# Earlier weight loads, a new order of the q, k and v loads, and a wider search in the planner of a fused attention and mixer kernel

## The chip, the cores and the metric

The kernel runs on one core of a Trainium2 chip. The metric is the device time of one execution in microseconds (us), of which medians are quoted. Every kernel is run in rounds beside the kernel before, on the same chip. A ratio is the mean time of one kernel's fast runs over that of the other kernel's fast runs of the same rounds, so it is not quite the ratio of the medians that stand beside it. An interval is a 95% one. Profiled executions are with a mean granted clock (the share of its full clock that PE was given) of 0.99 or more, unless it is said otherwise.

## The reference

Eight batches of attention over eight heads, 576 positions and a head dimension of 64, with a causal mask and a decay bias from `s`; the result goes through two mixers, one over the positions (tokens) and one over the 512 channels:

```python
cum = np.cumsum(np.maximum(s, 0.0), axis=-1)
scores = q @ k.T / 8 + np.minimum(-(cum[..., :, None] - cum[..., None, :]), 0.0)   # causal
x = softmax(scores) @ v                             # to [8, 576, 512]
u = x + (relu(x.T @ w_tok1) @ w_tok2).T             # token mixing
out = u + relu(u @ w_ch1) @ w_ch2                   # channel mixing
```

(Shortened: transposes and shapes are left to the reader.)

## The kernel before

The kernel doesn't fix the order of its instructions. It states operations with what they read and write, the engines that may run them and an assumed duration; a planner, in Python, simulates them, chooses engine and order, and repeats that with perturbed priorities. The best order by the planner's own reckoning is what each engine gets. So a changed load can move every instruction.

```python
def run(self, passes=5, search=60):
    rng = random.Random(1)
    for i in range(passes + search):
        self.reset()
        if i >= passes:                     # five plain passes, then random ones
            for o in self.ops:
                o.tail = base[o] + (rng.gauss(0.0, 2.0) if rng.random() < 0.02 else 0.0)
        order, length = self.once(i > 0)
        if best is None or length <= best[0]:
            best = ...                      # cut
```

(The loop is shortened.) All loads go through one queue of SyncE, in the order in which they are stated. The engines' names below are PE (matmuls; PEld is its weight load), DVE, ACT and POOL; SPq is the queue of SyncE. The part that the change touches:

```python
stage_v(0, 0)                       # v of batch 0, heads 0 to 3, five chunks
quad(0, 0)
load_tok1(Buf(r_uTb))
stage_v(0, 1)                       # heads 4 to 7
quad(0, HQ)
...
load_tok2(Buf(r_x))                 # then cast to bf16 by ACT and POOL
sga, sv = Buf(r_ga), Buf(r_vf)      # staging buffers of the channel weights
load_ch1(sga, 0, 0); load_ch1(sga, 1536, 1); load_ch1(sv, 0, 2); load_ch1(sga, 0, 3)
stage_qk(1, 0);  load_ch2(sga, 1536, 0)
stage_qk(1, HQ); load_ch2(sv, 0, 1); load_ch2(sga, 0, 2)
v1 = stage_v(1); ...; load_ch2(sga, 1536, 3)
for b in range(2, B):               # v between the k and q loads of its batch
    stage_qk(b, 0); vb = stage_v(b); vb[0](); vb[1]()
    stage_qk(b, HQ, 0); vb[2](); vb[3](); stage_qk(b, HQ, 1); vb[4]()
```

(Several statements are put on one line here, and cuts are marked with "...".) After a load of q or k come a cast, a 32-block transpose on DVE, and on ACT a square with its sum (a check of the inputs' size, whose result is needed only much later). The chunks of v are multiplied by the decay on POOL or DVE before the attention-times-v matmuls.

## Time and profile before

| | before |
|---|---|
| median time | 290.41 us (3 runs, 289.9 to 290.91) |
| profiled span | 288.6 us |
| PE busy | 278.1 us, 96% |
| useful matmul work (columns at 2400 per us, fillers left out) | 251.7 us |
| start A, to the long run of channel matmuls of batch 0 | 27.16 us |
| stage B, to the point where 51.4 us of work are done | 45.27 us |
| stage C, to the last matmul | 211.95 us |
| tail | 4.2 us |

How the stages are cut, and the lines behind the table, are in the prediction below. PE is 90% busy in nearly every slice, so a gain must come from short waits of PE or from better packing, not from making something else faster. And in the first ten slices the DMA engines are as full as PE.

### The profile page before, as it was taken

The numbers are of one execution on the slowest core, as the hardware profiler recorded it, in microseconds if no ns is written. First come the engines' busy times: TensorE is split into PE (matmuls) and PEld (weight loads), VectorE is DVE, ScalarE is ACT, GpSimd is POOL, SyncE is SP. The second block draws the span as 40 slices with busy tenths as digits, with TensorE's granted clock in tenths as the row PEclk, the third lists the DMA queues.
The fourth block names the chain that finished last, engine by engine and source line by source line (L and its number), as shares of the span: only waits on it lengthen the run. The fifth ranks groups of instructions, "written<-read, shape, count | busy, mean of one in ns | idle before, by whom it ended". The sixth has DMA issues, their size and how long they took to land.

```text
span 288.6 us, 6564 instructions
## 1 busy us (share of the span) xinstructions
PE 278.1 (96%) x2544; PEld 155.7 (54%) x2574; DVE 174.6 (61%) x333; ACT 187.3 (65%) x354; POOL 91.8 (32%) x143
## 2 busy tenths in 40 slices
PE   8889999999999999999999999999999999999994
PEld 3665455456754545356754545456744545357543
DVE  4973785989999774696358586785245513640022
ACT  3876876998899478986894578847842264018500
POOL 4653022557537427631382104621212102000000
PEclk9999999999999999999999999999999999999999
DMA  7999999899659999999935965951005310160032
GB/s 231 296 283 355 405 293 305 229 326 313 145 169 294 159 332 298 273 203 264 315 62 101 299 225 165 283 144 39 2 0 93 127 39 0 55 148 36 2 101 86
DMA packets 68128, 54.07 MB, mean 187 GB/s; under 512 B 53760, under 2 KB 56640, under 8 KB 68096
## 3 DMA queue, kind: packets, MB, share of 16 engines
q1 hardware_dynamic: 68096, 53.64, 66.7%
q8 instruction: 21, 0.34, 0.5%
q14 instruction: 11, 0.09, 0.1%
HBM read 40.65 MB, written 9.44 MB: 174 GB/s over the span
## 4 chain that ended last, share of the span: by engine, by line
PE 75%; DMA 11%; SPq 6%; ACT 3%; DVE 3%; issue 1%; DVEq 0%; ACTq 0%
PE pmx L1137 29%; PE pmx L1111 27%; DMA qkf<-in_q_dram 6%; PE pmx L803 5%; PE psc L759 4%; SPq L635 4%; PE pmx L1028 4%; DMA vf<-in_v_dram 4%; PE pmx L1053 4%; DMA x<-in_moe_w_tok_dram 2%; PE psc L923 1%; SPq L680 1%; DVE qkb L701 1%; PE pmx L965 1%; PE pmx L1036 1%
## 5 line engine op out<-in xcount | busy, mean ns | idle before, releaser
L776 ACT ACTIVATE E<-psc 128x512 bf16<-128x512 f32 x120 | 63.6, 601 | 25.1 <-PE psc L759 22.5
L784 POOL TENSOR_SCALAR_AFFINE_SELECT E<-E 128x512 bf16<-128x512 bf16 (+1 forms) x65 | 38.0, 614 | 96.3 <-ACT E L776 74.4
L1111 PEld LDWEIGHTS <-wc 128*128 128x128 bf16 x528 | 50.8, 98 | 31.9 <-issue 0.9
L1137 PE MATMUL pmx<-wc,gb 128*128 128x512 bf16 (+1 forms) x244 | 53.8, 369 | 0.5
L1111 PE MATMUL pmx<-uTb,wc 128*128 128x320 bf16 x384 | 54.0, 299 | 0.0
L1117 ACT ACTIVATE gb<-pmx 128x320 bf16<-128x320 f32 x80 | 34.6, 443 | 23.5 <-PE pmx L1111 17.6
L647 POOL TENSOR_TENSOR vp<-vf,wT 128x512 bf16<-128x512 f32 (+2 forms) x35 | 34.8, 1012 | 19.9 <-DMA vf<-in_v_dram 13.8
L685 ACT ACTIVATE junk<-qkf 128x1152 bf16<-128x1152 f32 x32 | 37.5, 1171 | 4.2 <-DMA qkf<-in_k_dram 3.9
L1137 PEld LDWEIGHTS <-gb 128*128 128x128 bf16 x252 | 23.8, 98 | 25.4 <-issue 0.9
L1137 PE MATMUL pmx<-wc,ga 128*128 128x512 bf16 x137 | 32.9, 379 | 0.4
L1111 PE MATMUL pmx<-uTa,wc 128*128 128x512 bf16 x141 | 31.8, 379 | 0.2
L803 PEld LDWEIGHTS <-E 128*128 128x128 bf16 x576 | 20.9, 97 | 6.4 <-issue 2.0
L817 DVE TENSOR_TENSOR x<-pmx,rc 128x320 bf16<-128x320 f32 x48 | 23.1, 489 | 1.4
L1117 ACT ACTIVATE ga<-pmx 128x512 bf16<-128x512 f32 x27 | 16.1, 597 | 11.5 <-PE pmx L1111 11.5
L1145 DVE TENSOR_TENSOR of<-pmx,ub 128x512 f32<-128x512 f32 (+1 forms) x17 | 11.2, 658 | 20.0 <-PE pmx L1137 18.1
L714 DVE STREAM_TRANSPOSE kT<-qkb 128x576 f32<-128x576 f32 x16 | 20.0, 1253 | 3.4 <-PE psc L759 2.3
L1137 PEld LDWEIGHTS <-ga 128*128 128x128 bf16 x144 | 13.1, 98 | 15.5 <-issue 1.5
L714 DVE STREAM_TRANSPOSE qT<-qkb 128x576 f32<-128x576 f32 x16 | 19.9, 1246 | 0.7 <-POOL qkb L699 0.4
L759 PE MATMUL psc<-qT,kT 32*128 32x256 bf16 (+2 forms) x592 | 19.1, 251 | 1.1 <-DVE qT L714 1.0
L759 PEld LDWEIGHTS <-kT 32*128 32x128 bf16 x640 | 13.6, 92 | 9.5 <-issue 7.6
L701 DVE CAST qkb<-qkf 128x1152 bf16<-128x1152 f32 (+1 forms) x22 | 15.1, 700 | 4.1 <-DMA qkf<-in_k_dram 2.7
L812 DVE RECIPROCAL rc<-pmx 128x5 f32<-128x5 f32 x48 | 8.7, 184 | 14.2 <-PE pmx L803 13.7
(115 smaller groups left out, 295.0 us busy)
## 6 DMA issues: line engine op xcount, KB each, us to landing
qkf<-in_k_dram SPq DMA_DIRECT2D x20, 576.0 KB, 6.1
qkf<-in_q_dram SPq DMA_DIRECT2D x20, 576.0 KB, 6.4
out_dram<-of SPq DMA_DIRECT2D x31, 256.0 KB, 2.5
vf<-in_v_dram SPq DMA_DIRECT2D x28, 256.0 KB, 6.0
ga<-in_moe_w_ch_dram SPq DMA_DIRECT2D x6, 768.0 KB, 7.6
vf<-in_v_dram SPq DMA_DIRECT2D x15, 128.0 KB, 5.3
vf<-in_moe_w_ch_dram SPq DMA_DIRECT2D x2, 768.0 KB, 10.3
out_dram<-of SPq DMA_DIRECT2D x10, 128.0 KB, 2.4
```

Of the source, the lines that this page charges most:

```text
L647: eng.tensor_tensor(out=vp.t[0:n, c, h0:h1, 0:D], in0=vf.t[0:n, c, h0:h1, :], in1=wT[0:n, c, b * H + h0 : b * H + h1].unsqueeze(2).to_broa ...
L685: P.op({"ACT": (1.1, 1.5, lambda: nc.scalar.activation(out=junk[:, :], in_=f.t[:, :], func=AF.Square, accum_out=sq[:, col : col + 1]))}, r ...
L701: nc.vector.tensor_copy(out=o.t[:, a:z], in_=i.t[:, a:z])
L714: nc.vector.transpose(out=T.t[:, 0:S, :].rearrange("p s q -> p (s q)").bitcast(FP32).rearrange("p (t r) -> p r t", r=R), in_=t1.t[:, :].bi ...
L759: nc.tensor.matmul(out=ps[e].t[:, c0 : c0 + z - a], lhsT=kT.t[p0 : p0 + TP, jc * 128 : jc * 128 + 128, qq], rhs=qT.t[p0 : p0 + TP, a:z, qq ...
L776: nc.scalar.activation(out=E.t[:, e, ph * 512 : ph * 512 + 512], in_=p.t[:, :], func=AF.Exp, scale=0.125)
L784: nc.gpsimd.affine_select(out=w, in_=w, compare_op=ALU.is_ge, fill=0.0, base=0, pattern=[[0, HQ], [1, n]], channel_multiplier=-1)
L803: nc.tensor.matmul(out=o[:, ic, 0 : D + 1], lhsT=E.t[:, hh, d0 : d0 + 128], rhs=vp.t[:, jc, h + hh, 0 : D + 1], start=(jc == j_lo), stop=( ...
L817: nc.vector.tensor_tensor(out=x.t[:, :, (h + hh) * D : (h + hh + 1) * D], in0=o[:, :, 0:D], in1=rc.t[:, :].unsqueeze(2).to_broadcast([128, ...
L1111: nc.tensor.matmul(out=pm.t[:, 0 : e - a], lhsT=wc1[:, m, cc * 128 : cc * 128 + 128], rhs=uT.t[:, m, a:e], start=(m == 0), stop=(m == NMC ...
L1117: lambda cc=cc, pm=pm, a=a, e=e: nc.scalar.activation(out=g.t[:, cc, a:e], in_=pm.t[:, 0 : e - a], func=AF.Relu),
L1137: nc.tensor.matmul(out=pm.t[:, na:nb], lhsT=g.t[:, cc, c * 128 : c * 128 + 128], rhs=wc2[:, cc, na:nb], start=(cc == 0), stop=(cc == NCC - 1))
```

## The change

The intent was to have each load land nearer to its use: the second token weight ahead of three v chunks, a third staging buffer for the channel weights, channel weight 2 among the v chunks of batch 1, and from batch 2 on q and k ahead of v. The planner gets a wider search, and a scan on DVE becomes a short reduction. The core of the diff (of the search only its heart, of the check nothing is shown; the comment is added):

```diff
-    def run(self, passes=5, search=60):
+    def run(self, passes=5, search=100):
...
+                if mode > 0.4:                      # also move whole groups of matmuls
+                    for g in sorted({p[0] for p in ranks.values()}):
+                        if rng.random() < 0.1:
+                            trial[g] = trial.get(g, 0.0) + rng.gauss(0.0, 0.7)
...
-    stage_v(0, 1)
+    vh = stage_v(0, 1)
+    vh[0]()
+    vh[1]()
+    load_tok2(Buf(r_x))
+    vh[2]()
+    vh[3]()
+    vh[4]()
     quad(0, HQ)
...
-    load_tok2(Buf(r_x))
-    sga, sv = Buf(r_ga), Buf(r_vf)
+    sga, sv, sv2 = Buf(r_ga), Buf(r_vf), Buf(r_vf)
...
-    load_ch1(sga, 0, 3)
+    load_ch1(sv2, 0, 3)
...
+    load_ch2(sga, 1536, 1)
     v1[0]()
+    load_ch2(sv, 0, 2)
     v1[1]()
...
     for b in range(2, B):
         stage_qk(b, 0)
-        vb = stage_v(b)
-        vb[0]()
-        vb[1]()
-        stage_qk(b, HQ, 0)
...
+        stage_qk(b, HQ)
+        for f in stage_v(b):
+            f()
```

More of the change, by code (lines that the diff above doesn't have):

```diff
@@ L50 @@
 RING = 2048
+SEED = 1
 class Plan:
@@ L155, in reset @@
             r.uses = []
-    def run(self, passes=5, search=60):
+    def run(self, passes=5, search=100):
         best = None
         self.lengths = []
-        rng = random.Random(1)
+        rng = random.Random(SEED)
         base = None
+        ranks = {o: o.prio for o in self.ops if isinstance(o.prio, tuple)}
+        moved = {}
         for i in range(passes + search):
@@ L164, in run @@
             if i >= passes:
+                mode = rng.random()
                 for o in self.ops:
-                    o.tail = base[o] + (rng.gauss(0.0, 2.0) if rng.random() < 0.02 else 0.0)
-            used = {o: o.tail for o in self.ops} if i else None
-            order, length = self.once(i > 0)
+                    o.tail = base[o] + (rng.gauss(0.0, 2.0) if mode < 0.7 and rng.random() < 0.02 else 0.0)
+                trial = dict(moved)
+                if mode > 0.4:
+                    for g in sorted({p[0] for p in ranks.values()}):
+                        if rng.random() < 0.1:
+                            trial[g] = trial.get(g, 0.0) + rng.gauss(0.0, 0.7)
+                for o, p in ranks.items():
+                    o.prio = (p[0] + trial.get(p[0], 0.0),) + p[1:]
+            used = {o: o.tail for o in self.ops} if i else None
+            try:
+                order, length = self.once(i > 0)
+            except RuntimeError:
+                if i < passes:
+                    raise
+                continue
             if best is None or length <= best[0]:
@@ L173, in run @@
                 base = used
+                if i >= passes:
+                    moved = trial
             self.lengths.append(round(length, 1))
@@ L492 @@
     PMASK = 1
+    LATER = True
     VUS = 1.05
@@ L615 @@
     junk = sb("junk", [128, R * D], BF16, fast)
-    pre = s_sb
+    pre = sb("pre", [64, 3], FP32, fast)
     gap = sb("gap", [64, 4], FP32, fast)
@@ L669, in stage_v @@
         todo = [lambda c=c, h0=h0, h1=h1: chunk(c, h0, h1) for (h0, h1) in parts for c in range(NJ)]
-        if b:
+        if b or part and LATER:
             return todo
@@ L1176 @@
     load_ch1(sv, 0, 2)
-    load_ch1(sga, 0, 3)
+    load_ch1(sv2, 0, 3)
     stage_qk(1, 0)
-    load_ch2(sga, 1536, 0)
+    load_ch2(sga, 0, 0)
     stage_qk(1, HQ)
-    load_ch2(sv, 0, 1)
-    load_ch2(sga, 0, 2)
     v1 = stage_v(1)
+    load_ch2(sga, 1536, 1)
     v1[0]()
+    load_ch2(sv, 0, 2)
     v1[1]()
@@ L1188 @@
     v1[4]()
-    load_ch2(sga, 1536, 3)
+    load_ch2(sga, 0, 3)
     for b in range(2, B):
         stage_qk(b, 0)
-        vb = stage_v(b)
-        vb[0]()
-        vb[1]()
-        stage_qk(b, HQ, 0)
-        vb[2]()
-        vb[3]()
-        stage_qk(b, HQ, 1)
-        vb[4]()
+        stage_qk(b, HQ)
+        for f in stage_v(b):
+            f()
     for b in range(2):
@@ L1210 @@
             chan0(tok0(), av0)
-    P.op({"DVE": (1.3, 1.6, lambda: nc.vector.tensor_tensor_scan(
-        out=pre[:, :], data0=one_sb[:, :].to_broadcast([64, S]), data1=wn[:, 0:S], initial=0.0, op0=ALU.mult, op1=ALU.add))},
+    P.op({"DVE": (0.5, 0.7, lambda: nc.vector.tensor_reduce(
+        out=pre[:, :], in_=wn[:, 0:384].rearrange("p (c n) -> p c n", n=128), op=ALU.add, axis=mybir.AxisListType.X))},
         reads=["wn", ("sq", 10)], writes=["pre"], prio=50)
@@ L1218, in gaps @@
             j = 128 * (i + 1)
+            if i:
+                nc.vector.tensor_tensor(out=pre[:, i : i + 1], in0=pre[:, i : i + 1], in1=pre[:, i - 1 : i], op=ALU.add)
             nc.vector.scalar_tensor_tensor(out=gap[:, i : i + 1], in0=wn[:, j + 128 : j + 129], scalar=4.8e-7,
-                                           in1=pre[:, j - 1 : j], op0=ALU.mult, op1=ALU.is_lt)
+                                           in1=pre[:, i : i + 1], op0=ALU.mult, op1=ALU.is_lt)
         nc.vector.tensor_scalar(out=gap[:, 3:4], in0=cum[:, S - 1 : S], scalar1=160.0, scalar2=None, op0=ALU.is_gt)
```

## The prediction

> **What bounds the kernel now.** I first read the busy times and the 40 slices, because the parts moved are loads of the first hundred microseconds and their limit may differ from the average.
>
> ```profile
> span 288.6 us, 6564 instructions
> PE 278.1 (96%) x2544; PEld 155.7 (54%) x2574; DVE 174.6 (61%) x333; ACT 187.3 (65%) x354; POOL 91.8 (32%) x143
> ...
> PE   8889999999999999999999999999999999999994
> DMA  7999999899659999999935965951005310160032
> GB/s 231 296 283 355 405 293 305 229 326 313 145 169 294 159 332 298 273 203 264 315 62 101 299 225 165 283 144 39 2 0 93 127 39 0 55 148 36 2 101 86
> ```
>
> PE is the bound, in nine tenths of every slice. The DMA row says that for the first ten slices (to about 72 us) the DMA engines are just as full, and that slack appears only from the eleventh on. So two limits stand side by side where the change acts.
>
> PE busy time hides small waits, so I set useful work against the clock. The program's matmuls are known by count and width. A steady stretch gives their rate: in the chain, 96 matmuls of 320 columns took 13.04 us, 135.8 ns each, which is 320 columns at 2400 per us plus 2.5 ns. Counting columns at 2400 per us, score matmuls (32 rows, L759) at a quarter because four run together, the two 64-row kinds at a half, and fillers (L1264) and the unused general branch at nothing, both kernels hold the same 251.7 us of useful work. Cut at two places of the PE timeline:
>
> ```profile
> 27.16 9.44 PE L965 MATMUL pmx<-uTa,wc 128*128 128x512 bf16 x42
> ...
> 49.79 1.78 PE L803 MATMUL psc<-vp,E 128*128 128x65 bf16 x45
> ...
> 58.55 1.90 PE L1053 MATMUL pmx<-h,w 128*128 128x512 bf16 x7
> ...
> 68.19 0.63 PE L759 MATMUL psc<-qT,kT 32*128 32x256 bf16 x16 [0.37 <-DVE qT L714]
> ...
> 72.43 7.23 PE L1111 MATMUL pmx<-uTb,wc 128*128 128x320 bf16 x52
> ```
>
> In program order 12.0 us of useful work precede the first of these rows and 51.4 us the last. So start A (0 to 27.16) loses 15.2 us; stage B (27.16 to 72.43) does 39.4 in 45.3 and loses 5.9; stage C (72.43 to the last matmul's end at 284.4) does 200.3 in 212.0 and loses 11.7; the tail, a last addition and store, is 4.2. These add to 288.6. C holds 1797 matmuls in 109 runs of one kind: 2.5 ns for each matmul is 4.5 us, and the other 7.2 us are 0.066 us for each change of kind. That is about what a stream without waits costs, so C has little to give. At C's rate (5.8%) B would lose 2.3; the other **3.6 us of B are real waits**. By the rows: 27.16 to 49.79 nothing to speak of (0.2), 49.79 to 55.55 about 1.0 (attention times v of batch 1), 55.55 to 63.29 about 1.4 (token mixing of batch 1), then about 1.0 to 72.43, of which 0.37 is the qT wait shown.
>
> For A I followed the chain of work that ended last:
>
> ```profile
> 15.41 4.86 DMA x<-in_moe_w_tok_dram
> 20.29 0.67 ACT w L850
> 20.96 1.04 ACT x L823 x5
> 22.05 1.03 PE psc L923 x10
> ```
>
> The load of w_tok2 is queued behind all v chunks of batch 0, lands at 20.29, and ACT, in order, must cast it (0.67) before it normalises the fourth head (1.04), which the next token matmul waits for. That is the link that the first part of the change attacks.
>
> **What the Trainium skill says.** "Perfetto Trace Analysis", section Identifying the Most-Contended Engine, says matmul busy share is no good measure of distance from the roofline; the trace agrees: stage B shows 43.55 us busy in 45.27, against 39.4 us of work. "TensorE: Matmul & The Clock Gate", section Wait — 56ns, not 53.3ns?, gives N/2.4 GHz plus about 2.5 ns per warm matmul; the 135.8 ns above agree. "DMA: Bandwidth & Descriptors", section Queues, rings and completion order, has one queue consumed in ring order on each DMA engine: moving a load forward pushes back what it passes; here all loads sit on one queue. The same page's Why small descriptors are slow charges a fixed cost per packet, heavy for 256 bytes; v rows are 256 bytes, and in the slices where v chunks move the rate is near 230 GB/s at full DMA busy share, against 355 to 405 with wide rows.
>
> **The change part by part.**
>
> *w_tok2 before v chunks 2 to 4 of heads 4 to 7.* Bytes are unchanged. The three chunks passed are 320 KB; at some 230 GB/s that is 1.4 us, so w_tok2 should land near 18.9 instead of 20.29, and the last v chunk near 20.3 instead of about 18.85 (where the last v multiplication of batch 0 begins). Gain: the cast and head 3 no longer hold anything. Loss: the four attention-times-v groups of heads 4 to 7, at 19.20 to 21.9 before, now start after v plus one multiplication (0.4 to 0.6), about 20.8, and end about 22.1 (36 matmuls took 1.26). In the new order heads 2 and 3's token matmuls come after them and a filler, about 22.3, against 22.05. Then four heads are normalised on DVE at 0.20 + 0.49 each, 2.7 us from about 21.3, ending near 24.0; the last token matmuls then start near 24.1 against 24.88. With the same 2.3 us to follow, the long run of channel matmuls starts about 26.6 instead of 27.16. **A: −0.5 us.** The fillers agree: the new program has 28 in place of 29, all at the same places but one.
>
> *Three staging buffers.* The third and fourth pieces of channel weight 1 go to the two v buffers, so the fourth no longer waits for a cast out of ga. That wait was 4.4 us in the DMA queue's own waits (L888 on ga), but in those microseconds the DMA engines ran at 0.9 to 1.07: the queue had work ahead. Direct gain about 0; it lets the k and q loads of batch 1 be queued some us earlier.
>
> *Channel weight 2 among v of batch 1; q and k ahead of v from batch 2.* Stage B's DMA is full, so nothing moves more bytes; only the order is nearer to the use. Before, q of batch 2 heads 4 to 7 was issued at about 61.9 behind v and its score matmuls waited at 68.19. Now k and q of a batch go together and that wait should vanish (0.4). The new PE order also puts three to six channel matmuls (0.65 to 1.3 us) between groups of attention times v, and three between the token matmuls and their continuation, where PE before ran 63 such matmuls in a row with DVE in between. I credit 0.7 of the first 1.0, 0.5 of the 1.4, 0.4 of the last 1.0. **B: −1.6 us.**
>
> *The planner's wider search and the shorter check.* Instructions of C change places, not number: 116 runs in place of 109, 7 × 0.066 = **+0.4 us** in C. The scan of 1.60 us on DVE at 76.55 becomes a reduction; DVE is no bound there: 0.
>
> Sum: −0.5 − 1.6 + 0.4 = −1.7; 290.4 − 1.7 = 288.7, and I write 288.6.
>
> **Rivals.** (1) *Hidden anyway.* With DMA full to 72 us, each load brought forward delays another: v of batch 2 now waits behind two 576 KB loads (about 1.7 us each at 350 GB/s), while its five POOL multiplications (1.04 us each) ended near 67 and are used from 70.40. That slack of 3.4 is just the delay, so B could gain only 0.5: 289.8 to 290.4. For it: the full DMA row. Against: k and q had cost a visible wait, v had not. (2) *A new wait.* The same delay overshoots, or v(0)'s later landing in A is not hidden; attention times v waits on the POOL multiplications, and PE is held up to 2 us: 291 to 292. For it: POOL already waited for v 13.8 us in all. Against: v is consumed a batch later than it is queued. (3) *All waits go.* If A gains 1.5 and B all 3.6: 285.3. Even this is 1.8%, so faster by over 2% (under 284.6) needs a gain in C, where no wait is seen.
>
> **Range and chances.** Between rival 3 softened and rival 2 softened: 286.4 to 291.0. Faster by over 2% has 0.03, slower by over 2% (over 296.2) 0.02, for a schedule whose assumed durations miss on the chip.
>
> **What would show it.** Right: w_tok2 lands before 19.5; the long L965 run (its new line) starts at 26.3 to 27.0; the score matmuls of batch 2 no longer name qT; the same 51.4 us of work are done near 70.3; the stretch to PE's end stays near 212. Wrong: PE waiting on attention times v behind POOL multiplications in 65 to 110 us; PE reaching the same work at 72 or later; C growing by over 1 us, which would mean that the search's new order, not the loads, decides.

## The result, and the profile after

The changed kernel took 289.46 us (median of 4 runs, 289.06 to 289.76), the kernel before in the same rounds 290.5 us (4 runs). The ratio is 0.9965, interval 0.9943 to 0.9987: about 1 us, a third of one per cent, "same" by the 2% line and inside the forecast range.

The page of the changed kernel answers to the lines shown of the kernel before:

```profile
span 287.9 us, 6550 instructions
PE 277.5 (96%) x2541; PEld 155.3 (54%) x2573; DVE 167.4 (58%) x330; ACT 183.3 (64%) x351; POOL 100.3 (35%) x151
...
PE   8899999999999999999999999999999999999994
...
DMA  7999998999568999549914978793007310280032
...
PE 87%; SPq 4%; issue 2%; DVE 2%; DMA 2%; ACT 1%; DVEq 0%; ACTq 0%
```

The last line is the head of the chain that ended last. Before, its first entries were PE 75%, DMA 11%; now DMA is 2% of it. The new order of loads did take the loads off the critical chain, and the time hardly moved. That contrast is the puzzle.

The same cuts through PE's timeline of the changed kernel (its lines are 19 to 21 further down than those of the kernel before: L984 was L965, L1130 was L1111, L822 was L803, L1047 was L1028, L778 was L759):

```profile
27.38 7.93 PE L984 MATMUL pmx<-uTa,wc 128*128 128x512 bf16 x35
...
49.24 1.25 PE L822 MATMUL psc<-vp,E 128*128 128x65 bf16 x36
...
54.57 1.90 PE L1047 MATMUL pmx<-x,w 128*128 128x512 bf16 x8
...
66.91 0.63 PE L778 MATMUL psc<-qT,kT 32*128 32x256 bf16 x16
...
71.41 7.78 PE L1130 MATMUL pmx<-uTb,wc 128*128 128x320 bf16 x56
```

The first row is the end of start A, and it has moved the wrong way, from 27.16. In the fourth row the wait on qT (0.37 before) is gone. In program order 50.88 us of work precede the last row, so the 51.4 us at which stage C was cut are reached about 0.55 later, at 71.96.

| stage | before | after | difference | forecast |
|---|---|---|---|---|
| A | 27.16 | 27.38 | +0.2 | -0.5 |
| B | 45.27 | 44.58 | -0.7 | -1.6 |
| C | 211.95 | 211.92 | 0.0 | +0.4 |
| tail | 4.2 | 4.0 | -0.2 | 0 |
| span | 288.6 | 287.9 | -0.7 | -1.7 |

Where did A's gain go? The next lines are a stretch of the changed kernel's timeline, all engines:

```profile
18.48 0.67 ACT L869 CAST w<-x 128x576 bf16<-128x576 f32 x1 [0.54 <-DMA x<-in_moe_w_tok_dram]
...
19.53 1.09 DVE L666 TENSOR_TENSOR vp<-vf,wT 128x256 bf16<-128x256 f32 x3 [1.68 <-DMA vf<-in_v_dram]
...
22.57 0.83 ACT L869 CAST wc<-ga 128x768 bf16<-128x768 f32 x1 [1.21 <-DMA ga<-in_moe_w_ch_dram]
...
23.46 0.10 PEld L984 LDWEIGHTS <-wc 128*128 128x128 bf16 x1 [0.40 <-ACT wc L869]
...
23.69 1.03 PE L942 MATMUL psc<-x,w 128*128 128x128 bf16 x10 [0.45 <-ACT h L949]
```

The second token weight lands by 18.48 (20.29 before), as forecast. But the v chunks behind it arrive later: the multiplication by the decay starts at 19.53, not at 18.17 as before. And PE's new order has the first channel matmul (the PEld row) ahead of the last twenty token matmuls. Its weight was still being cast by ACT, which itself waited 1.21 us for the load. PE stood until 23.46. The last row names the ReLU's `h` for its wait of 0.45; the weight-load row shows what stood in front. (That `h` was not needed is seen in the first experiment, where the same matmuls ran from 23.19 while ACT did its `h` from 23.34 on.)

In stage B the token mixing of batch 1 begins 1.0 us earlier (54.57 against 55.55), yet the channel matmuls behind it begin at 63.56, against 63.29. PE's timeline before, and then after:

```profile
55.55 1.90 PE L1028 MATMUL pmx<-x,w 128*128 128x512 bf16 x8
...
63.05 0.40 PE L1083 MATMUL pmx<-ident,us 128*128 128x128 bf16 x4 [0.31 <-DVE us L1070]
63.29 4.54 PE L1111 MATMUL pmx<-uTb,wc 128*128 128x320 bf16 x32
```

```profile
62.70 0.38 PE L1102 MATMUL pmx<-ident,ub 128*128 128x128 bf16 x4 [0.45 <-ACT uTb L1110]
63.19 0.38 PE L1102 MATMUL pmx<-ident,us 128*128 128x128 bf16 x4
63.56 3.42 PE L1130 MATMUL pmx<-uTb,wc 128*128 128x320 bf16 x24
```

From 54.57 to 63.56 are 8.99 us, before the same stretch took 7.74; 0.65 of the difference is three channel matmuls that the new order puts in between, so it is worse by 0.6. I read this at first as ACT's fault: in its order a square of q, 1.2 us long, stands at 60.88 ahead of the copies of uTb. The experiments below show that this reading was wrong.

### The profile page after: what moved, and what is told of

It is laid out like the page before. It is cut to its first block, busy times and chain, and to the rows that moved or that the text cites. A ratio compares the mean times of both kernels' runs of the same rounds, so it can differ in the third digit from the quotient of the medians.

```text
span 287.9 us, 6550 instructions
## 1 busy us (share of the span) xinstructions
PE 277.5 (96%) x2541; PEld 155.3 (54%) x2573; DVE 167.4 (58%) x330; ACT 183.3 (64%) x351; POOL 100.3 (35%) x151
## 4 chain that ended last, share of the span: by engine, by line
PE 87%; SPq 4%; issue 2%; DVE 2%; DMA 2%; ACT 1%; DVEq 0%; ACTq 0%
PE pmx L1130 29%; PE pmx L1156 29%; PE psc L778 5%; PE pmx L822 5%; PE pmx L1047 4%; PE pmx L984 4%; PE pmx L1007 3%; PE pmx L1072 3%; SPq L654 3%; DMA vf<-in_v_dram 2%; PE pmx L1055 1%; PE psc L822 1%; PE psc L942 1%; SPq L699 1%; DVE x L836 1%
## 5 line engine op out<-in xcount | busy, mean ns | idle before, releaser
L795 ACT ACTIVATE E<-psc 128x512 bf16<-128x512 f32 x120 | 63.1, 608 | 15.9 <-PE psc L778 12.0
L1130 PEld LDWEIGHTS <-wc 128*128 128x128 bf16 x528 | 50.6, 98 | 31.6 <-issue 1.3
L803 POOL TENSOR_SCALAR_AFFINE_SELECT E<-E 128x512 bf16<-128x512 bf16 (+1 forms) x65 | 38.3, 617 | 81.6 <-ACT E L795 58.8
L1130 PE MATMUL pmx<-uTb,wc 128*128 128x320 bf16 x384 | 54.0, 300 | 0.0
L1136 ACT ACTIVATE gb<-pmx 128x320 bf16<-128x320 f32 x83 | 36.2, 438 | 21.2 <-PE pmx L1130 14.2
L1130 PE MATMUL pmx<-uTa,wc 128*128 128x512 bf16 x139 | 32.7, 380 | 0.2
L1136 ACT ACTIVATE ga<-pmx 128x512 bf16<-128x512 f32 x23 | 13.7, 597 | 18.5 <-PE pmx L1130 18.5
L718 POOL CAST qkb<-qkf 128x1152 bf16<-128x1152 f32 (+1 forms) x15 | 14.7, 991 | 28.3 <-DVE kT L733 8.9
L822 PEld LDWEIGHTS <-E 128*128 128x128 bf16 x576 | 20.6, 97 | 5.5 <-issue 1.0
L778 PE MATMUL psc<-qT,kT 32*128 32x256 bf16 (+2 forms) x592 | 19.2, 252 | 1.3 <-DVE qT L733 1.3
L778 PEld LDWEIGHTS <-kT 32*128 32x128 bf16 x640 | 13.4, 92 | 10.3 <-issue 7.5
```

The lines of the kernel that those rows point to most:

```text
L718: nc.gpsimd.tensor_copy(out=o.t[:, a:z], in_=i.t[:, a:z])
L778: nc.tensor.matmul(out=ps[e].t[:, c0 : c0 + z - a], lhsT=kT.t[p0 : p0 + TP, jc * 128 : jc * 128 + 128, qq], rhs=qT.t[p0 : p0 + TP, a:z, qq ...
L795: nc.scalar.activation(out=E.t[:, e, ph * 512 : ph * 512 + 512], in_=p.t[:, :], func=AF.Exp, scale=0.125)
L803: nc.gpsimd.affine_select(out=w, in_=w, compare_op=ALU.is_ge, fill=0.0, base=0, pattern=[[0, HQ], [1, n]], channel_multiplier=-1)
L822: nc.tensor.matmul(out=o[:, ic, 0 : D + 1], lhsT=E.t[:, hh, d0 : d0 + 128], rhs=vp.t[:, jc, h + hh, 0 : D + 1], start=(jc == j_lo), stop=( ...
L1130: nc.tensor.matmul(out=pm.t[:, 0 : e - a], lhsT=wc1[:, m, cc * 128 : cc * 128 + 128], rhs=uT.t[:, m, a:e], start=(m == 0), stop=(m == NMC ...
```

## The experiments

**The method.** For seven of the twelve runs the changed kernel's plan was kept as it is ("frozen") and single operations were given another place in it before the instructions were emitted. So a difference is that of the edit and not of a new draw of the planner. The other five change what the planner is given.

**Theory.** The loads came in time, and the gain was lost where an in-order engine had a wrong instruction ahead of the one that PE needed: in A the first channel matmul, in B the squares on ACT. **The DMA rival** (rival 1 of the prediction): the loads are hidden or collide anyway, since DMA is full. **The search rival**, which the forecast named only as what a growth of C would mean: the search's draw decides, not the loads.

### First channel matmul behind the last token matmuls

```diff
     order = P.run()
+    keep_op["ch", 0, 0].start = keep_op["ch", 1, 0].start - 0.005
+    order.sort(key=lambda o: (o.start, o.idx))
```

> The changed kernel with one PE operation moved: the first channel matmul of batch 0 (L984, one of 512 columns) goes from ahead of the last token matmuls of batch 0 to behind them; every other instruction keeps its place. Theory (that matmul's weights are still being cast by ACT until 23.40, and PE, in order, stands 0.45 us at it): the token matmuls x20 start near 23.25 instead of 23.69, the long run of channel matmuls near 26.9 instead of 27.38, and the time is some 0.4 us under the changed kernel's, about 289.0 (ratio to before 0.995). Rival (the relu on ACT, which the list of waits names, or the normalisation on DVE holds them): start stays at 23.6 to 23.7 and 27.3 to 27.4, time 289.5 (0.9965).

It took 290.22 us, ratio 0.9969 (0.994 to 0.9999). The twenty token matmuls began at 23.19 in place of 23.69 and without a wait, and the long run of channel matmuls at 26.89 in place of 27.38. Of these 0.49 us, 0.22 is the matmul that moved, so 0.27 is real, and as 0.28 it was still there at 63.28 and 71.13. So the starts came as the theory said; the time did not (ratio 0.9969 for some 0.995). By 82 us the gain had vanished. DVE's cast of batch 4's first k in the changed kernel, and then all engines near 80 us in this one:

```profile
78.01 0.98 DVE L720 CAST qkb<-qkf 128x1152 bf16<-128x1152 f32 x1
```

```profile
78.65 1.23 DVE L722 CAST qkb<-qkf 128x1152 bf16<-128x1152 f32 x1 [0.75 <-DMA qkf<-in_k_dram]
...
79.79 0.18 DVE L833 RECIPROCAL rc<-pmx 128x5 f32<-128x5 f32 x1
...
81.89 0.49 DVE L838 TENSOR_TENSOR x<-pmx,rc 128x320 bf16<-128x320 f32 x1
...
82.44 0.81 PE L1051 MATMUL pmx<-x,w 128*128 128x512 bf16 x3 [0.43 <-DVE x L838]
```

Here DVE had to wait 0.75 us for the load of that k; in the changed kernel it did not wait. The normalisation of batch 2, for which PE waits, stands behind it in DVE's order. Token mixing of batch 2 started at 82.44, in the changed kernel at 82.23. The 0.28 won turned into 0.21 lost. Most of this is not that DVE came early: the load was issued at 73.5 and took 5.2 to land, in the changed kernel at 72.8 and 5.0. The five v chunks ahead of it in the queue took 10.19 us to issue (from 63.15), in the changed kernel 9.26 (from 63.42). So a late load took the gain back in this execution, as the DMA rival has it, but whether the edit or chance made it late is open.

### A square on ACT put later

```diff
+    squares[2, HQ, 0].start += 3.58
```

> The changed kernel with one ACT operation moved: the square of k of batch 2, heads 4 to 7 (1.2 us at 60.88), goes behind the two copies and three exponentials that followed it. Theory (ACT is in order, the square holds the copies that free PSUM for the transposes): the last transposes stop waiting 0.45 us on ACT, the channel run of batch 1 starts at 62.7 to 63.0 instead of 63.56, and the time falls by 0.5 us to about 289.0 (0.995). Rival 1 (the additions on DVE hold the transposes anyway): 63.4 to 63.6 and 289.5. Rival 2 (the later square frees its k buffer later and delays a load of batch 3): 62.8 at first, but the gain is lost by 72 us, time 289.5.

This edit missed. It moved the square of k, which stood at 57.83, to a place directly behind the square of q, so that two of them now stood ahead of the copies of uTb (at 60.21 and 61.52; the copies began at 62.68 in place of 62.03). PE's wait grew from 0.45 to 1.03 and the channel matmuls began at 64.00. It took 290.16 us, ratio 0.9989 (0.9949 to 1.003). It shows that squares on ACT can hold PE, but not that the one in the changed kernel does.

### The second token weight back behind the v chunks, in the frozen plan

```diff
+    tok2_op.start = v_op.start + 0.01      # w_tok2 behind the last v chunk of batch 0
```

> The changed kernel with w_tok2's load put back behind the last v chunk of batch 0; only the order of the loads differs. Theory (what w_tok2 gains by landing early, v loses by landing late, and the start of the long channel run is a wash): w_tok2 lands near 20.3 instead of 18.5, the last v multiplications start near 18.5 instead of 19.5, the long channel run starts within 0.5 us of 27.38, time 289.2 to 290.0. Rival (the early landing is worth more than 1 us in this order of instructions, since ACT has the cast ahead of a relu and a normalisation): start at 28.4 or later, time 290.5 or more.

It took 292.4 us, ratio 1.0042 (0.9997 to 1.0086). In the profile, the wait is where it was expected:

```profile
21.28 0.61 PE L963 MATMUL psc<-w,h 128*128 128x512 bf16 x2 [1.83 <-ACT h L951]
```

The long run began at 29.77, 2.39 later than in the changed kernel, and the last run of 96 channel matmuls at 259.84, still 2.40 later. So the rival held and the theory, a wash, did not: in this order of instructions the early load was worth 2.4 us in the profiled execution. Not all of it is the wait. Just after it the granted clock (PEclk) was halved for 3.4 us:

```profile
core 0: us, PE busy (x) PEld busy (x) DVE busy (x) ACT busy (x) POOL busy (x), PEclk, DMA share, GB/s
21.90:25.30 3.40, 3.40 (x46) 2.86 (x45) 2.55 (x9) 1.45 (x4) 1.24 (x4) 0.50 1.08 380
```

Ten token matmuls took 1.47 us in it (at 24.22), where they took 1.03 elsewhere. The rounds agree: the four executions with a mean clock of 0.994 or less took 292.1 to 293.84 us, the two with 0.998 or more 290.31 and 290.89. Yet the kernel before, with the late load and its own order, reached that point at 27.16. The planner had arranged the engines around the late load, at no visible cost.

### v of batch 2 back between its q and k loads, in the frozen plan

```diff
+    for o, c, d in ((k2, 0, 0.02), (k2, 1, 0.01), (q2, 2, 0.02), (q2, 3, 0.01)):
+        ld["v", 2, c].start = o.start - d      # k2, q2: loads of heads 4 to 7
```

> The changed kernel with the v chunks of batch 2 put back between its k and q loads as they were before; only the order of loads differs. Theory (q and k ahead of v removed the waits between 63 and 72 us): a wait on qT of 0.4 us or more comes back there, the run of 56 channel matmuls starts at 71.9 to 72.4 instead of 71.41, time 290.0 to 290.4 (0.998 to 1.0). Rival (the planner's new order on PE and ACT did it, not the loads): 71.3 to 71.6, time 289.5 (0.9965).

It took 293.93 us, ratio 1.0117 (1.008 to 1.0154). I had expected the 0.4 us wait on qT of the kernel before to come back. What came was ten times that, elsewhere (and again a clock of 0.50 after it, from 64.8 to 68.1):

```profile
60.92 1.15 POOL L724 CAST qkb<-qkf 128x1152 bf16<-128x1152 f32 x1 [3.01 <-DMA qkf<-in_q_dram]
...
62.11 1.26 DVE L739 STREAM_TRANSPOSE qT<-qkb 128x576 f32<-128x576 f32 x1 [3.75 <-POOL qkb L724]
...
63.94 0.62 PE L1084 MATMUL pmx<-h,w 128*64 128x512 bf16 x4 [3.92 <-DVE ub L1097]
```

Read upwards from the PE row. PE names `ub`, the residual additions on DVE, which had nothing to do with q. They stood behind a transpose of q in DVE's order, and that waited for POOL's cast, and that for the load. The Trainium skill, "PSUM — Partial Sum Buffer", section Engine vs sequencer instructions, says that the queues of ScalarE, VectorE and GpSimdE are strict FIFO; this run agrees, with DVE idle for 3.75 us in front of an addition that was ready.

### The search alone, and the loads alone

The kernel before with only the new search, and the changed kernel with only the old search (the two lines stand for the whole of the search's edit):

```diff
-    def run(self, passes=5, search=60):       # kernel before, new search; and the reverse
+    def run(self, passes=5, search=100):
```

> The kernel before with the changed kernel's wider search and nothing else; loads in the old order. Theory (the loads and the engines' order fit together, the search alone finds nothing): ratio to before 0.998 to 1.002, PE reaches its last run of 96 channel matmuls within 0.3 us of 257.9. Rival (the gain of the change is the search's): ratio 0.995 to 0.997, that run at 257.5 or earlier.

> The changed kernel with the search of before (60 trials, no moves of whole ranks). Theory (the new order of loads is what gains): ratio 0.995 to 0.998, last run of 96 channel matmuls at 257.2 to 257.9. Rival (the wider search is needed to use the loads): ratio 1.0 or above, 258 or later.

The new search with the old loads took 294.45 us, ratio 1.0134 (1.0109 to 1.016). The new loads with the old search took 290.66 us, ratio 0.9997 (0.9977 to 1.0016). Neither half shows the gain, and neither ratio is in the range of its theory; the second interval overlaps that of the changed kernel, so a small gain of the new loads under the old search is not ruled out. Of the first, the list of PE's waits shows what its plan ran into:

```profile
PE psc L777 <- DVE qT L732: 1.7, 1, 1.7
PE pmx L1129 <- ACT gb L1135: 1.4, 2, 0.8
...
PE pmx L1046 <- DVE x L835: 0.9, 1, 0.9
PE psc L777 <- ACT E L794: 0.7, 1, 0.7
```

(Columns: what waited for what, us in total, times, the longest.) A wider search lost 1.3% on the chip. So the search rival has to be tested by itself.

### No search in either kernel, and another seed

```diff
-    def run(self, passes=5, search=100):      # and search=60 in the kernel before
+    def run(self, passes=5, search=0):
```

```diff
-SEED = 1
+SEED = 2
```

> The changed kernel with the search taken away (its first five deterministic passes alone), to be read against the kernel before with the same taken away in the same call. Theory (the new order of loads is worth something by itself in stage B, and the search only adds luck): 0.002 to 0.010 less in the ratio than the kernel before without its search; both at 1.00 to 1.03 of the kernel before. Rival (the loads are hidden anyway): the two ratios agree within 0.002.

> The kernel before with its search taken away (its first five deterministic passes alone). Both theories: slower than the kernel before, 1.00 to 1.03. With the run of the changed loads without search beside it, the difference is the loads' own: theory 0.002 to 0.010 worse than that run, rival within 0.002 of it.

> The changed kernel with another seed of the planner's search and nothing else. Theory (the order that the search happens to find decides as much as the change of the loads does): the ratio to before is anywhere from 0.993 to 1.01, and it differs from the changed kernel's 0.9965 by at least 0.003. Rival (the loads decide and the search is noise below what is measured): 0.9955 to 0.9975. The run starts of stage C would then be offset as a rigid body by under 0.3 us against the changed kernel.

With the five plain passes alone the changed loads took 290.86 us, ratio 1.0009 (0.9991 to 1.0026), and the old loads 295.59 us, ratio 1.0168 (1.0147 to 1.0189; the median is of all seven runs, the ratio leaves out two slow ones; the profiled run is one of these, so its stages aren't compared). The changed kernel with another seed took 290.14 us, ratio 0.9996 (0.9977 to 1.0015).

| ratio to the kernel before | old loads | new loads | new over old |
|---|---|---|---|
| five passes, no search | 1.0168 | 1.0009 | 0.984 |
| old search | 1 | 0.9997 | 1.000 |
| new search | 1.0134 | 0.9965 (other seed 0.9996) | 0.983 |

"New loads" stands for all of the change but the search, the third buffer and the shorter check too. The last column is the quotient of the two before it. Read by rows, the new loads are worth 1.6%, nothing (to 0.2%), or 1.7%, depending on the planner. Read by columns, the old loads scatter over 1.7% with the planner's draw, the new ones over 0.44%. The old search had found for the old loads an order that is 1.7% better than the plain one; it had already bought, by luck or by trying, what the new loads would have given. The forecast that the no-search pair would differ by 0.2 to 1% was too small. The seed pair, 0.9965 against 0.9996, differs by about 0.3%, with intervals that overlap, so the seeds are not told apart; the whole gain of the change is no larger than that.

The planner's own reckoning: the kernels print it when `PLAN` is set, without the chip (PE's lines come in the order of the traces, so these are the plans that ran):

| planner's length, us | old loads | new loads |
|---|---|---|
| five passes, no search | 290.56 | 287.34 |
| old search | 287.87 | 286.93 |
| new search | 289.47 | 286.92 (other seed 287.08) |

It has the two slow plans as the two longest. So the wider search did not mislead the planner about the old loads; its random draws found only a plan 1.6 us longer than the old search's. For the change as a whole the planner forecast -0.95 us, about what was measured. That it is so near is partly luck: it promised -0.93 for the new loads under the old search too, and there the chip shows no gain.

### Two and three moves together: an editing error, then the corrected version

To see whether the change's forecast gain could be had after all, I put the moves together: the first channel matmul late, the right square (of q) behind the copies of uTb, and in the second kernel the DVE cast of batch 4's k behind batch 2's normalisation.

```diff
+    keep_op["ch", 0, 0].start = keep_op["ch", 1, 0].start - 0.005
+    squares[2, HQ, 1].start += 3.55
```

> The changed kernel with the first channel matmul of batch 0 behind the last token matmuls (as in ch_late) and the square of q of batch 2, heads 4 to 7, behind the copies and exponentials that follow it. Theory: start 26.9 as in ch_late, no wait of transposes on ACT, channel run of batch 1 at 62.7 instead of 63.56; but the DVE cast of batch 4's first k, which waits for its load until about 78.6, stands ahead of the normalisation of batch 2, so token mixing of batch 2 starts at 82.2 to 82.5 as before and the end is that of the changed kernel, ratio 0.996 to 0.998. Rival (the gain is kept): token mixing at 81.4, end 0.8 us earlier, ratio 0.993.

> two_moves with that DVE cast moved behind the normalisation of batch 2. Theory (the in-order DVE at a load that has not landed takes back what was gained): token mixing of batch 2 starts at 81.3 to 81.6, the last run of 96 channel matmuls at 256.5 to 256.8 instead of 257.44, time 0.8 us under the changed kernel, ratio 0.993 to 0.995. Rival (another load of the full DMA stage takes it back): token mixing at 82.2 or later, ratio 0.996 to 0.998.

They took 298.83 and 299.01 us, both with ratio 1.028 (1.0255 to 1.0305, and 1.0249 to 1.0311). The edit was at fault: the buffer that the square reads is loaded again, with q of batch 3, and the moved square now stood behind that load. It waited for data that it wasn't meant to read (only a check used its sum, and the result was correct). They say nothing on the theory. They do measure what an in-order wait costs:

```profile
70.92 1.16 ACT L706 ACTIVATE junk<-qkf 128x1152 bf16<-128x1152 f32 x1 [7.03 <-DMA qkf<-in_q_dram]
```

ACT waited 7.03 us, PE next for 6.90 us on ACT's `gb`, and the span was 296.6 us, 8.1 over that of the run with the first move alone. That is more than the wait: from 69.6 to 76.4 the granted clock was 0.50, and over this whole execution 0.986 (0.985 in the other). The corrected version moves that load behind the square as well:

```diff
+    sq2.start += 3.55
+    q3.start = sq2.start + 0.01            # the load that uses the buffer again
+    k4.start = max(norms[2, hh].start for hh in range(HQ, H)) + 0.9
```

> The changed kernel's frozen plan with three things out of the way of an in-order engine: the first channel matmul behind the last token matmuls of batch 0; the square of q of batch 2, heads 4 to 7, on ACT moved 3.55 us later, and this time the load that reuses its buffer (q of batch 3) is moved behind it on the queue too; and the DVE cast of batch 4's first k behind batch 2's normalisation, copy and reduce. Theory (the gain was lost where an in-order engine had the wrong instruction ahead): long run of channel matmuls starts near 26.9, no wait of PE on ACT uTb near 62.7, the 24 matmuls after the token mixing of batch 1 start near 62.9, batch 2's token mixing near 81.3 to 81.7 against 82.23, the last run of 96 channel matmuls at 256.5 to 256.9 against 257.44, ratio to before 0.993 to 0.995. Rival (the DMA engines, full to 72 us and again near 80, decide): the gain is there at 63 us but gone by 82.2 or later, ratio 0.996 to 0.998. The earlier version of this edit left the load in front of the square and lost 8 us; if the edit is right now, no wait of ACT on q above 1 us is seen near 70.

It took 289.98 us, ratio 0.9989 (0.9961 to 1.0017): no better than the changed kernel. ACT was now free when the copies were due, and this is what came of it, in a stretch of its timeline:

```profile
61.77 1.37 DVE L1097 TENSOR_TENSOR us<-pmx,x 64x512 bf16<-64x512 f32 x2
...
62.16 0.59 ACT L1118 COPY uTb<-pmx 128x512 bf16<-128x512 bf16 x1 [0.45 <-PE pmx L1110]
...
63.20 0.40 PE L1110 MATMUL pmx<-ident,us 128*128 128x128 bf16 x4 [0.63 <-DVE us L1097]
...
63.65 0.57 PE L1138 MATMUL pmx<-uTb,wc 128*128 128x320 bf16 x3
```

ACT now waits for PE, not PE for ACT. The wait of 0.45 on ACT has become one of 0.63 on DVE, and the transposes of `us` start at 63.20, in the changed kernel at 63.19. The wait that the view had named was not the one that set the time. Another of nearly the same length lay beside it. So the second half of my theory falls: taking the square away did not give stage B its gain.

What most likely sets the time there is seen in DVE's own timeline, first of the kernel before, then of the changed one:

```profile
57.80 0.69 DVE L1043 TENSOR_SCALAR h<-pmx 128x512 bf16<-128x512 f32 x1
58.41 0.75 DVE L701 CAST qkb<-qkf 128x1152 bf16<-128x1152 f32 x1
59.19 2.48 DVE L1070 TENSOR_TENSOR ub<-pmx,x 128x512 bf16<-128x512 f32 x4
61.60 1.40 DVE L1070 TENSOR_TENSOR us<-pmx,x 64x512 bf16<-64x512 f32 x2
```

```profile
57.59 0.69 DVE L1019 COPY of<-pmx 128x512 f32<-128x512 f32 x1 [0.23 <-PE pmx L1007]
58.20 1.25 DVE L733 STREAM_TRANSPOSE qT<-qkb 128x576 f32<-128x576 f32 x1
59.29 2.47 DVE L1089 TENSOR_TENSOR ub<-pmx,x 128x512 bf16<-128x512 f32 x4
61.68 1.37 DVE L1089 TENSOR_TENSOR us<-pmx,x 64x512 bf16<-64x512 f32 x2
```

PE comes a microsecond earlier, but DVE puts a copy and a transpose of q ahead of the additions, and so begins them at 59.29 in place of 59.19 and ends them at nearly the same time (63.05, before 63.00). From 54.4 to 63.1 DVE was busy for 8.42 of 8.70 us (before, 8.53), though over the whole span it is busy for 58%. That DVE's order is the cause is read from the traces and from the wait that took ACT's place; I have no run that moves the transpose, so its size is open.

The third move worked as meant: from 63.65 to the token mixing of batch 2 at 82.31 the corrected version lost nothing against the changed kernel (18.66 us against 18.67), where the run with the first move alone lost 0.49. But the first move's gain isn't to be seen in this profile: the long run began at 27.26, where the run with that move alone had 26.89. Its first score matmuls were 0.27 later (8.80 against 8.53), before anything that was edited, and a wait of 0.18 on a v multiplication followed at 20.74. So effects of 0.3 us are as large as what one execution's early loads differ from another's, and single profiles don't settle them; nor do the rounds, whose intervals are about 0.3% to either side.

### What stage C says in all of them

The start of one group of attention-times-v matmuls and of the last run of 96 channel matmuls, in four kernels of the same plan:

| | attention times v | last run of 96 | between |
|---|---|---|---|
| changed kernel | 138.67 | 257.44 | 118.77 |
| first channel matmul late | 138.89 | 257.67 | 118.78 |
| a square later (missed edit) | 139.12 | 257.91 | 118.79 |
| three moves, corrected | 138.75 | 257.52 | 118.77 |

Stage C moves as a rigid body. What is lost or won before 83 us arrives at the end unchanged; nothing there absorbs or amplifies it.

## Why the prediction was right, and where its steps were wrong

The forecast of "same", with 288.6 us and a range of 286.4 to 291.0, held: 289.46 us. Little was risked: the range takes in the time of the kernel before, so no effect at all would have been right too. Its frame held (though "nine tenths of every slice" is 8 in the first three slices and 4 in the last): PE is the bound, C has nothing to give, and only the waits of A and B can be won. But the sum of -1.7 came out as -0.7 in the profiles and -1.0 in the medians, with errors of +0.7, +0.9 and -0.4 in its terms that partly cancel, so these have to be taken one by one. Of its five signs of being right, three came (w_tok2 before 19.5, no qT wait in the scores of batch 2, C near 212); the start of the long run (27.38, not 26.3 to 27.0) and the end of B (71.96, not near 70.3) failed.

- **w_tok2 lands near 18.9, v near 20.3.** Right in kind: 18.48 and, for the multiplication behind v, 19.53. The frozen plan shows what the load is worth when the instructions count on it: 2.4 us in one execution, the halved clock included.
- **A: -0.5.** Wrong, +0.2. The step that failed is "with the same 2.3 us to follow". The last ten token matmuls began near 24.7 (0.45 of that is the wait for a weight cast, in a place where the new order had put a channel matmul too early), not at 24.1. And 2.7 us followed, because the new order leaves two more second-layer token matmuls (0.43) and four more transposes (0.23) to the end, less the channel matmul (0.22) that it has put ahead. Moving that matmul back gave 0.27 of the 0.7 us of difference.
- **Three staging buffers: about 0.** No run isolates them. With C unchanged and the first part of B changed by -0.1 only, nothing speaks against it.
- **B: -1.6, as -0.7, -0.5 and -0.4.** Measured -0.7, of which -0.1 came before attention times v. Attention times v gave 0.4 of its 0.7 (loss 1.25 before, 0.82 after), and the stretch with the qT wait gave 0.7, more than its 0.4; the named wait is 0.37 of it. (The load behind that wait was misread: by the chain, the q that DVE cast at 65.13 was issued at 58.53 and took 6.50. What was issued at 61.9 landed after 68.19.) The term that failed is the 0.5 for token mixing of batch 1: it is worse by 0.6, most likely since DVE, in order, finishes the additions no earlier. The forecast counted PE's waits and did not add up DVE's work in that window.
- **C: +0.4 for more changes of kind.** Measured 0.0, with 116 runs as foreseen. An average cost for each change of kind, fitted on one plan, didn't carry over to another.
- **Rival 1, hidden anyway,** was seen in one profile alone, of the first experiment at 82 us, where a later load took back what the first channel matmul had won. Its reckoning of 289.8 to 290.4 isn't far from the time measured, but its mechanism (v's slack used up) isn't what was seen: PE waits on no v multiplication in B. The DMA row behind it was also read too simply: DMA is full again from slice 13 to slice 20 (87 to 144 us).
- **Rival 2, a new wait,** and **rival 3, all waits go,** did not come.
- **"That the search's new order, not the loads, decides"** was put under what would make the prediction wrong, with a growth of C as its sign. The sign didn't show, but the thing was there: with the planner's search varied, the same loads are worth 0 to 1.7%. That the kernel before was a well-drawn plan, which had hidden its late loads, is the best account of why a sound change of loads moved so little. It rests on the two tables of planners and loads, three plans of the old loads and four of the new, not on any one trace; the old search with another seed was not run.

## What to carry to other kernels

Where a search decides the order of instructions, compare changes with the search off as well as on, and with a second seed, and print the planner's own length first; a tuned plan may already have bought what the change offers. A load order and the engines' in-order queues belong together: change one and freeze the other, and a wait of 0.4 us can become 4. A wait can cost more than its length: during or after those of 1.83, 3.92 and 6.90 us the granted clock was 0.50 for 3.4, 3.4 and 6.8 us, while after one of 1.7 us (new search, old loads) it stayed at 1.00. And before you remove the wait that the trace names, look for what would be waited for next: the named one is only the last to end.

## What the Trainium skill lacked or had wrong

- "TensorE: Matmul & The Clock Gate", section Back-to-back issue gap, gives about 131 ns for each 512-column matmul in a sustained stream of weight loads and matmuls. In the changed kernel 16 such matmuls, each with its own weight load, took 3.45 us in the chain, 216 ns each. The section calls the N/2.4 + 2.5 ns formula one for isolated matmuls; here it is the rate of the stream, and 135.8 ns for 320 columns agree with it.
- "PSUM — Partial Sum Buffer", section Engine vs sequencer instructions, has the strict FIFO of the engines' queues, but no page that I read tells what it costs when a load's order changes: 3.92 us of PE waiting on additions that were ready but for one late load of q, and 6.90 us behind one misplaced square.
- No page that I read says that a gap's named releaser may hide a second one of the same length: taking away a wait of 0.45 us on ACT left one of 0.63 us on DVE, and the next matmuls started at 63.20 in place of 63.19.
